# Last feature rows of the plain steps from one slot, spread copies placed in other steps, and shape order of odd tiles in a spectral-plus-MLP layer

## Chip, core and metric

The kernel runs on one core of a Trainium2 chip. The metric is the device time of one launch in microseconds; of several runs the median counts. The engines are TensorE (PE; its weight loads are listed apart as PEld), VectorE (DVE), ScalarE (ACT), GpSimd (POOL), and SyncE (SP), whose queue issues the transfers.

## What is computed

`x` has 2048 rows of 576 features, all in float32. Cut to what matters:

```python
x = A_x                                         # (1, 2048, 576)
X = rfft2(layernorm(x)) * (w_r + 1j * w_i)      # over rows and features
h = x + irfft2(X, s=(2048, 576))
h2 = h + relu(layernorm(h) @ w1) @ w2           # w1: 576 x 4608, w2: 4608 x 576
```

## The kernel before

The two-dimensional transform is written as products with constant matrices. The rows are split into 16 tiles of 128 rows, and the work runs in stages.

**Stage one** takes a tile `t` at a time. DVE measures mean and variance (`stat1`, `aggr1`, `row1`), POOL raises the variance to the power -0.5 (`pow1`), DVE and POOL fold the tile into sums and differences (`add1`, line 263, on DVE; `sub1`, line 258, on POOL), ACT scales the constants by the tile's deviation (`scale1`: line 267 writes one column, line 268 the 192 columns of constants), and PE multiplies (`fwd_a`): eight products of 128x128 and then four of 64x64 (`rest`). ACT evicts the result (line 159). The helpers `mm` and `act` record every product as line 156 and every copy or scaling on ACT as line 159. Tile 15 alone does its 64x64 products first, into a PSUM buffer of its own that DVE evicts (line 285). The loop runs over 18 steps; `fwd_a` follows two steps behind the statistics, so that in the order of ACT the scaling of a tile stands behind the eviction of the tile two before it.

**Stage two** (`mid_*`) does the small transforms and the spectral multiplication. **Stage three** goes back (`inv_*`), adds `x` (line 519), normalises again (`stat2`, `norm2`), and `project(t)` transposes each normalised tile, which makes the operands of the MLP. Its order is written out by hand in `STEPS`: a letter names a function, the number its argument, `A` and `B` are the two halves of a plain MLP step, and steps with `=` are jobs of a queue of sums and transfers.

The MLP works in float32 products of rounded high and low parts: w*x is taken as wh*xh + wh*xl + wl*xh. The rows are in four chunks of 512 (`CH` = 4 tiles), whose operands lie in `xc[c]` (tiles named B for chunks 0 and 1, C for chunk 2, X for chunk 3), with ten slots of 512 columns. The 576 features are 4 x 128 + 64, and slot 2 holds the 64 left over: their high part in partitions 0 to 63, the low part in 64 to 127. **Plain steps** (`mm1`, then `mm2`) take one group of 256 hidden units and one chunk. In `mm1` each 128 hidden units take 14 products: twelve for four blocks of 128 features and two for the last 64, one of which reads slot 2 and one slot 5. Slot 5 is filled by copies inside the chip, and they also move 32 partitions within slot 2: the last `project` of a chunk issues on SP four copies (line 579) and, behind their landing, a fifth (line 580). The **double steps** later on (Strassen's scheme over groups and chunk pairs, `l1_prod`, `second`, `slot`) read slots 0 to 2 and 3 to 5 as the two halves of the features.

Plain steps 3 to 8 run in a loop over `i` and `q`, with the table `JOBS` for what else is issued at each place (`L` loads, `S` sums, `H`, `I`, `W`, `X` splits, `K` stores). The first weights of the double steps are loaded by `load_w1` (lines 333 and 335) and `load_w2`; POOL makes their low parts (line 353) and the Strassen sums (lines 749 to 752).

## Time and profile before

| | before |
|---|---|
| median of 3 runs | 965.67 us (965.51 to 966.04) |
| profiled execution | 965.46 us |
| its span, first to last instruction | 963.7 us |
| busy: PE, PEld | 955.7 us (99%), 850.1 us (88%) |
| busy: DVE, ACT, POOL | 770.6 (80%), 466.7 (48%), 646.1 us (67%) |
| chain that ended last, by engine | PE 96%, DVE 1%, DMA 1%, ACT 1%, the rest under 1% |
| granted clock of TensorE, mean | 0.999 of full speed |

Between the span and the execution's own time lie 1.8 us. The busy share of an engine counts every instruction from its start to its end; the chain is followed back from the last instruction to what released it, step by step. A busy PE may still hold small gaps between its instructions, which the timeline shows.

### The profile page before, as it was taken

The page shows a single profiled execution, that of the slowest core. Times are in us where ns is not written, and L with a number is a line of the kernel's source. Part 1 is how long each engine was busy: PE and PEld are TensorE (multiplying, and loading weights), DVE is VectorE, ACT ScalarE, POOL GpSimd, SP SyncE. Part 2 cuts the span into 40 slices and gives each one's busy share as a digit, 9 for nine tenths or more (in the row PEclk, how much of TensorE's full clock was granted, in tenths as well). Part 3 has the DMA queues.
Part 4 walks back from the last instruction along what each step waited for, and adds up shares of the span by engine and source line. Part 5 has one row for each costly group of instructions (what it writes and reads, how often), then busy time and mean ns, then how long its engine had stood idle before and what let it go on. Part 6 is the DMA issues. An engine that isn't in the chain of part 4 may idle for free.

```text
span 963.7 us, 18094 instructions
## 1 busy us (share of the span) xinstructions
PE 955.7 (99%) x6658; PEld 850.1 (88%) x6658; DVE 770.6 (80%) x1226; ACT 466.7 (48%) x912; POOL 646.1 (67%) x783
## 2 busy tenths in 40 slices
PE   9999999999999999999999999999999999999997
PEld 7777778999988999999999999999999999999997
DVE  8577996687768888887888888888878888878886
ACT  6544558323355454545445444554554545444441
POOL 7213787514788777878686878767787768687842
PEclk9999999999999999999999999999999999999999
DMA  7974727557639264563728091836456372819365
GB/s 205 237 188 111 183 97 261 170 205 256 212 118 326 90 238 145 185 199 129 257 71 302 29 325 45 284 98 231 152 176 207 122 262 66 303 35 318 103 213 154
DMA packets 122840, 176.09 MB, mean 183 GB/s; under 512 B 7552, under 2 KB 102400, under 8 KB 122752
## 3 DMA queue, kind: packets, MB, share of 16 engines
q1 hardware_dynamic: 121584, 173.61, 55.9%
q10 hardware_dynamic: 1168, 1.33, 0.4%
q8 instruction: 53, 0.87, 0.4%
q14 instruction: 35, 0.29, 0.1%
HBM read 150.53 MB, written 23.07 MB: 180 GB/s over the span
## 4 chain that ended last, share of the span: by engine, by line
PE 96%; DVE 1%; DMA 1%; ACT 1%; issue 0%; SPq 0%; POOL 0%
PE h L826 36%; PE d L931 35%; PE d L156 24%; DMA C<-C 1%; PE d L564 1%; PE h L931 0%; DMA X<-in_A_x_dram 0%; DVE st L242 0%; ACT X L159 0%; ACT e L159 0%; ACT C L159 0%; DVE A L941 0%; DVE e L414 0%; DVE e L415 0%; DVE A L937 0%
## 5 line engine op out<-in xcount | busy, mean ns | idle before, releaser
L941 DVE TENSOR_TENSOR A<-A,d 128x576 f32<-128x576 f32 x428 | 317.5, 752 | 84.1 <-PE d L931 71.2
L931 PE MATMUL d<-X,D 128*128 128x288 f32 x1476 | 224.3, 294 | 0.1
L931 PEld LDWEIGHTS d<-X,D 128*128 128x128 f32 x1476 | 211.0, 188 | 10.5 <-DVE A L941 0.3
L826 PE MATMUL h<-B,e 128*128 128x512 f32 x658 | 166.8, 392 | 0.0
L159 ACT ACTIVATE e<-h 128x512 f32<-128x512 f32 x93 | 55.6, 597 | 188.0 <-PE h L826 187.9
L826 PEld LDWEIGHTS h<-B,e 128*128 128x128 f32 x658 | 118.3, 188 | 20.4
L353 POOL TENSOR_TENSOR e<-e,e 128x512 fp32r<-128x512 f32 (+3 forms) x68 | 89.8, 1320 | 57.9 <-ACT e L159 55.3
L642 ACT ACTIVATE e<-e 128x512 f32<-128x512 f32 x93 | 58.8, 633 | 107.5 <-DVE e L884 45.2
L826 PE MATMUL h<-X,e 128*128 128x512 f32 x434 | 110.0, 392 | 0.0
L353 POOL TENSOR_TENSOR X<-e,X 128x576 fp32r<-128x576 f32 (+1 forms) x34 | 49.9, 1469 | 62.8 <-ACT X L159 60.7
L826 PEld LDWEIGHTS h<-X,e 128*128 128x128 f32 x434 | 78.0, 188 | 13.4
L159 ACT ACTIVATE e<-e 128x256 fp32r<-128x256 f32 (+5 forms) x171 | 78.6, 489 | 14.3 <-DVE e L673 6.1
L850 POOL TENSOR_TENSOR A<-e 128x256 f32<-128x256 f32 x61 | 48.0, 787 | 28.4 <-DVE X L840 25.3
L840 DVE TENSOR_TENSOR D<-A,D 128x512 fp32r<-128x512 f32 x61 | 63.3, 1038 | 1.7 <-ACT D L159 1.7
L931 PEld LDWEIGHTS d<-X 128*128 128x128 f32 x372 | 55.6, 188 | 5.3 <-issue 0.4
L931 PE MATMUL d<-X 128*128 128x288 f32 x372 | 58.9, 294 | 0.1
L931 PE MATMUL d<-X,e 128*128 128x288 f32 x360 | 57.1, 294 | 0.0
L826 PE MATMUL h<-F,e 128*128 128x512 f32 x217 | 55.0, 392 | 0.0
L852 POOL TENSOR_TENSOR A<-e,A 128x256 f32<-128x256 f32 x61 | 52.9, 867 | 0.8 <-DVE A L848 0.8
L156 PE MATMUL d<-e,D 128*128 128x288 f32 x384 | 53.3, 295 | 0.0
L826 PE MATMUL h<-C,e 128*128 128x512 f32 x210 | 53.3, 393 | 0.0
L156 PEld LDWEIGHTS d<-e,D 128*128 128x128 f32 x384 | 51.9, 188 | 1.4 <-DVE A L632 0.4
(174 smaller groups left out, 1850.9 us busy)
## 6 DMA issues: line engine op xcount, KB each, us to landing
X<-t0T SPq DMA_DIRECT2D x16, 768.0 KB
X<-t1T SPq DMA_DIRECT2D x16, 768.0 KB
e<-in_B_w_dram SPq DMA_DIRECT2D x18, 576.0 KB
e<-in_B_w_dram SPq DMA_DIRECT2D x18, 512.0 KB
X<-t0T SPq DMA_DIRECT2D x16, 512.0 KB
X<-t1T SPq DMA_DIRECT2D x16, 512.0 KB
B<-t1T SPq DMA_DIRECT2D x8, 768.0 KB
B<-t1B SPq DMA_DIRECT2D x8, 768.0 KB
```

The lines of the kernel that those rows point to most:

```text
L156: nc.tensor.matmul(o, l, r, start=start, stop=stop)
L159: nc.scalar.activation(o, i, AF.Copy, **kw)
L353: eng.tensor_sub(l, v, h)
L564: nc.tensor.transpose(pz[:, 128 * ORDER[b]:128 * ORDER[b] + 128], y[:, 128 * b:128 * b + 128], ident)
L642: nc.scalar.activation(o, i, AF.Relu)
L826: nc.tensor.matmul(o, a, b, start=bool(first) and n_ == 0, stop=n_ == len(ops) - 1, skip_group_check=not first)
L840: (eng or nc.vector).tensor_sub(f[1], v, f[0])
L850: nc.gpsimd.tensor_sub(s3, p0[:, :256], p0[:, 256:])
L852: nc.gpsimd.tensor_sub(s4, p1_[:, :256], s2)
L931: nc.tensor.matmul(P[tt], l[:, q], r, start=first and n_ == 0, stop=end and n_ == 2, skip_group_check=whole and not first)
L941: nc.vector.tensor_add(xt, xt, P)
```

## The change

Four places are edited. (1) In stage one the odd tiles issue their 64x64 products ahead of the 128x128 ones. (2) The last tile's statistics, fold and scaling are issued in step 15 of the loop instead of step 16, and its subtraction by DVE instead of POOL. (3) The two products of `mm1` for the last 64 features both read slot 2; the weights of these features are therefore loaded twice, into partitions 0 to 63 and 64 to 127, their high part is made by one copy on ACT, and the low part is followed by zeros. That takes two transfers instead of three and no memset. Group 2 (`FIRST`), which serves plain and double steps, loads both forms. (4) The spread copies leave `project` and become jobs: `F0`, `F1`, `F3` fill slot 5 of a chunk, `G0` moves the 32 partitions within slot 2 of chunk 0, and the five copies of chunk 2 are issued at step (`END` - 1, 2). `project` is told which engine takes its 64-row subtraction: POOL for tiles 0 to 7, DVE for the others (before, tiles 3 and 7 were DVE's too).

```diff
@@ -22,6 +22,7 @@
 GF = 2
 NG = DFF // (128 * GF)
 CH = 4
+FIRST = 2
 NC = NT // CH
 WARM = 25
 APART = 3
@@ -254,8 +255,8 @@
         r = first(t)[4]
         nc.gpsimd.tensor_tensor(r[:, 1:2], r[:, 0:1], half[:, :1], op=ALU.pow)
 
-    def sub1(t):
-        nc.gpsimd.tensor_sub(dims(first(t)[0], 575, [1, 2], [-2, 144]), *pair(t))
+    def sub1(t, eng=nc.gpsimd):
+        eng.tensor_sub(dims(first(t)[0], 575, [1, 2], [-2, 144]), *pair(t))
 
     def add1(t):
         G, _, _, _, r = first(t)
@@ -283,13 +284,15 @@
             p2 = ps()
             rest(p2)
             nc.vector.tensor_copy(dims(zx, 8192 + 2 * t, [32, 64], [1, 2]), dims(p2, 256, [1, 64], [512, 2]))
+        elif t % 2:
+            rest(p)
         for h in range(2):
             for k in range(2):
                 for j in range(2):
                     q = slice(64 * j, 64 * j + 64)
                     mm(p[:, 512 * j + 128 * h:512 * j + 128 * h + 128], dims(G[q], (k, 321 - k)[h], [2, 128]),
                        caf[q, 64 * k:64 * k + 128], k == 0, k == 1)
-        if not end:
+        if t % 2 == 0:
             rest(p)
         act(dims(zx, 2 * t, [2048, 5 - end], [32, 64], [1, 2]), dims(p, 0, [64, 5 - end], [1, 64], [512, 2]))
 
@@ -301,7 +304,7 @@
     warm_pe(WARM)
     sub1(0)
     for t in range(NT + 2):
-        old = 1 <= t <= NT
+        old = 1 <= t < NT
         if old and t <= 2:
             row1(t - 1)
             pow1(t - 1)
@@ -315,12 +318,18 @@
             stat1(t, 1)
         if old and t > 2:
             add1(t - 1)
-        if 1 <= t < NT:
+        if 1 <= t < NT - 1:
             sub1(t)
         if t < NT:
             aggr1(t)
-        if old:
+        if 1 <= t < NT:
             scale1(t - 1)
+        if t == NT - 1:
+            row1(t)
+            pow1(t)
+            add1(t)
+            sub1(t, nc.vector)
+            scale1(t)
         if t >= 2:
             fwd_a(t - 2)
 
@@ -328,9 +337,16 @@
     nc.sync.dma_start(c3t, c3)
     raw, wts = {}, {}
 
+    def load_rest(g, v):
+        for k in range(2):
+            nc.sync.dma_start(v[64 * k:64 * k + 64], w1[512:576, 256 * g:256 * g + 256])
+
     def load_w1(g, v1, v4):
         f = slice(256 * g, 256 * g + 256)
         nc.sync.dma_start(v1, w1[0:512, f].rearrange("(a p) f -> p a f", p=128))
+        if g < FIRST:
+            load_rest(g, v4)
+            return
         for k in range(3):
             nc.sync.dma_start(v4[32 * k:32 * k + 32], w1[512:576, f].rearrange("(h p) f -> p h f", p=32))
 
@@ -368,9 +384,12 @@
         rest = [v[:, 1024:] for v in r]
         wts[g, 0] = h, l, rest
         v1, _, v4 = raw[g]
+        if g == FIRST:
+            v4 = vs["v4"]
         split(h, l, v1, nc.gpsimd)
-        for k in range(2):
-            split_rest(rest[k], v4[:, k], nc.gpsimd)
+        act(rest[0], v4)
+        nc.gpsimd.tensor_sub(rest[1][:64], v4[:64], rest[0][:64])
+        nc.gpsimd.tensor_sub(rest[1][64:], rest[0][64:], rest[0][64:])
 
     def split_rest(o, v, eng=nc.vector):
         act(o, v)
@@ -462,7 +481,7 @@
         if step[0] == "l":
             mid_l(k, k + 1)
         elif step[0] == "L":
-            load_weights(0, leftover())
+            load_weights(0, sb([128, 512], "G")[:, :256])
         elif step[0] == "W":
             warm_pe(k)
         else:
@@ -557,7 +576,7 @@
             nc.scalar.activation(z[:, i, :D], xs[:, t0 + i, :], AF.Identity, bias=r[2][:, 2, i:i + 1], scale=r[2][:, 1, i:i + 1])
         act(z[:, :, D:], z[:, :, 512:D])
 
-    def project(t):
+    def project(t, eng):
         y = Zs.pop(t)
         pz = ps()
         for b in range(5):
@@ -571,20 +590,20 @@
         nc.sync.dma_start(xd[t], zt)
         for h in range(2):
             nc.gpsimd.tensor_sub(dst[:, 6 + 2 * h:8 + 2 * h, q], zt[:, 384 * h:384 * h + 256].rearrange("p (a s) -> p a s", s=128), dst[:, 3 * h:3 * h + 2, q])
-        made[t // CH] += 1
-        (nc.gpsimd if t < 8 and made[t // CH] < CH else nc.vector).tensor_sub(dst[64:, 2, q], zt[64:, 256:384], dst[64:, 2, q])
-        if made[t // CH] == CH:
-            u = dst.bitcast(F32)
+        eng.tensor_sub(dst[64:, 2, q], zt[64:, 256:384], dst[64:, 2, q])
+
+    def spread(c, half):
+        u = xc[c].bitcast(F32)
+        if half:
             for a, b in ((0, 32), (32, 32), (64, 96), (96, 96)):
                 nc.sync.dma_start(u[a:a + 32, 5], u[b:b + 32, 2])
+        else:
             nc.sync.dma_start(u[32:64, 2], u[0:32, 2])
 
     ORDER = (0, 1, 3, 4, 2)
-    made = [0] * 4
     xd = {}
     hid, pend = {}, {}
     steps = [(0, 0), (0, 1), (0, 2), (1, 1), (0, 3), (1, 3), (1, 0), (1, 2), (2, 3), (2, 2)]
-    FIRST = 2
     END = len(steps) - 1
 
     ring = []
@@ -606,7 +625,7 @@
         for kt in range(4):
             x = kt + kt // 2
             ops += [(w1h[:, kt, f], x), (w1h[:, kt, f], 6 + kt), (w1l[:, kt, f], x)]
-        ops += [(rest[h][:, f], 3 * h + 2) for h in range(2)]
+        ops += [(rest[h][:, f], 2) for h in range(2)]
         for n_, (w, x) in enumerate(ops):
             mm(p, w, xc[c][:, x, :], n_ == 0, n_ == len(ops) - 1)
         if i < APART:
@@ -1057,17 +1076,15 @@
         "h1 h0 S1 d1 o1 d0 o0 S0 h3 h9 d9 d3 r1 h2 e0 h6 e1 h4 s0 s1 d4 o3 d2 d6 n0 o6 h10 o2 h7 d10 d7 j1 o7 r2 "
         "e2 h11 h5 h12 e3 s2 s3 d5 j0 o4 o5 d12 d11 r4 n2 h13 e6 e7 d13 s6 o10 j2 o11 j3 h8 r3 e5 e4 h14 d8 d14 "
         "s7 s4 s5 r6 e11 o9 h15 n6 o12 o14 o13 d15 A0 o8 e10 n4 A1 o15 j6 s10 j4 j5 B0 r5 e9 r7 e8 e13 e12 j7 "
-        "s11 B1 B2 s8 s9 r8 e15 s12 =K0 n10 e14 s14 T n8 s13 B3 A10 =L0 j10 A11 j9 j11 j8 B10 s15 n12 =L1 B11 V0 "
-        "B12 B13 n14 =P0 j13 j12 A20 =S0 V1 A21 j14 A30 =S1 j15 =L2 =L3 A31 B20 =P1 B21 =H0 B22 =W0 =H1 B23 =W1 "
-        "=S2 "
+        "s11 B1 B2 s8 s9 r8 e15 s12 =F0 =F1 =K0 n10 e14 s14 T n8 s13 B3 A10 =L0 J10 A11 J9 J11 J8 B10 s15 n12 =L1 "
+        "B11 V0 B12 B13 n14 =P0 J13 J12 A20 =S0 V1 A21 J14 A30 =S1 J15 =L2 =L3 A31 B20 =P1 =F3 B21 =H0 B22 =W0 =H1 "
+        "B23 =W1 =S2 "
     )
 
     def tail_in():
         tail.append(sb([128, 10752], "X", dt=F32R))
         xc.append(tail[0][:, :5120].rearrange("p (a n) -> p a n", a=10))
-        v4 = ebuf([128, 2, 256])
-        nc.gpsimd.memset(v4, 0.0)
-        load_weights(1, v4)
+        load_weights(1, ebuf([128, 256]))
         groups.extend(sum_jobs(k // CH, k % CH, v) for k, v in enumerate("ABCABABA"))
 
     groups, stage, FT = [], [], {}
@@ -1089,20 +1106,20 @@
 
     JOBS = (
         "L4 / H2 I0 I1 / W2 X0 X1 / S3 L5 I2 / X2 H3 I3 / W3 X3 K1 / S4 L6 / "
-        "H4 I4 / W4 X4 / S5 L7 / H5 I5 / W5 X5 / S6 / H6 I6 / W6 X6 / S7 / H7 I7 / W7 / X7"
+        "H4 I4 / W4 X4 / S5 L7 / H5 I5 / W5 X5 / S6 / G0 H6 I6 / W6 X6 / S7 / H7 I7 / W7 / X7"
     ).split(" / ")
 
     def job(name, k):
         if name in "LSHIWX":
             groups[k][name]()
         else:
-            dict(K=keep_block, P=sum_bufs)[name](k)
+            dict(K=keep_block, P=sum_bufs, F=lambda c: spread(c, 1), G=lambda c: spread(c, 0))[name](k)
 
     def work(k):
         for v in JOBS[k].split() if 0 <= k < len(JOBS) else ():
             job(v[0], int(v[1:]))
 
-    CALLS = dict(h=inv_h, d=inv_d, o=inv_o, r=inv_r, e=inv_e, s=stat2, n=lambda t: norm2(t, 2), j=project,
+    CALLS = dict(h=inv_h, d=inv_d, o=inv_o, r=inv_r, e=inv_e, s=stat2, n=lambda t: norm2(t, 2), j=lambda t: project(t, nc.gpsimd), J=lambda t: project(t, nc.vector),
                  A=lambda k: mm1(*divmod(k, 10)), B=lambda k: mm2(*divmod(k, 10)), T=lambda k: tail_in(),
                  S=lambda k: split_weights(0, k), V=lambda k: split_weights(1, k))
     for step in STEPS.split():
@@ -1126,7 +1143,10 @@
                 TF["T4"] = TS[:, 0:3], TS[:, 3:5]
             work(4 * i + q - 12)
             if (i, q) == (4, 3):
-                vs[1], vs[2], vs[4] = raw[FIRST] = ebuf([128, 4, 256]), ebuf([128, 2, D]), leftover()
+                e = ebuf([128, EW])
+                vs["v4"] = e[:, 1024:]
+                vs[1], vs[2], vs[4] = raw[FIRST] = e[:, :1024].rearrange("p (a b) -> p a b", a=4), ebuf([128, 2, D]), leftover()
+                load_rest(FIRST, vs["v4"])
                 load_w1(FIRST, vs[1], vs[4])
             if (i, q) == (5, 2):
                 load_w2(FIRST, vs[2])
@@ -1141,6 +1161,9 @@
                 w2_sums()
             if (i, q) in ((END - 2, 3), (END - 1, 0)):
                 w2_split(("T34", "T12")[q == 3], nc.gpsimd)
+            if (i, q) == (END - 1, 2):
+                spread(2, 1)
+                spread(2, 0)
             if i == END - 1:
                 if q == 0:
                     w1_sums(0)
```

Three places in the order of the instructions follow, before and after. The first is PE in stage one, tiles 0 to 3; `d` is the tile's PSUM buffer, `e` its folded rows.

```order
L156 MATMUL d_236<-e_200 128x128 x8
L156 MATMUL d_236<-e_200 64x64 x4
L156 MATMUL d_264<-e_212 128x128 x8
L156 MATMUL d_264<-e_212 64x64 x4
L156 MATMUL d_292<-e_226 128x128 x8
L156 MATMUL d_292<-e_226 64x64 x4
L156 MATMUL d_320<-e_250 128x128 x8
L156 MATMUL d_320<-e_250 64x64 x4
```

After the change, at the same place:

```order
L157 MATMUL d_236<-e_200 128x128 x8
L157 MATMUL d_236<-e_200 64x64 x4
L157 MATMUL d_264<-e_212 64x64 x4
L157 MATMUL d_264<-e_212 128x128 x8
L157 MATMUL d_292<-e_226 128x128 x8
L157 MATMUL d_292<-e_226 64x64 x4
L157 MATMUL d_320<-e_250 64x64 x4
L157 MATMUL d_320<-e_250 128x128 x8
```

Only the two pieces of the odd tiles (d_264, d_320) have changed places; the tiles themselves keep their order.

The second is ACT at the end of stage one, before. `A<-d` is an eviction (of tiles 12 to 15 here), `e<-X,r` and `e<-cc,r` are the two scalings of a tile (14 and 15).

```order
L159 ACTIVATE A_173<-d_572 128x320x2
L267 ACTIVATE e_558<-X_66,r_86_561 128x1
L268 ACTIVATE e_558<-cc_76,r_86_561 128x192
L159 ACTIVATE A_173<-d_600 128x320x2
L267 ACTIVATE e_586<-X_66,r_91_589 128x1
L268 ACTIVATE e_586<-cc_76,r_91_589 128x192
L159 ACTIVATE A_173<-d_620 128x320x2
L159 ACTIVATE A_173<-d_634 128x256x2
```

And after:

```order
L160 ACTIVATE A_173<-d_572 128x320x2
L268 ACTIVATE e_558<-X_66,r_86_561 128x1
L269 ACTIVATE e_558<-cc_76,r_86_561 128x192
L268 ACTIVATE e_586<-X_66,r_91_589 128x1
L269 ACTIVATE e_586<-cc_76,r_91_589 128x192
L160 ACTIVATE A_173<-d_606 128x320x2
L160 ACTIVATE A_173<-d_620 128x320x2
L160 ACTIVATE A_173<-d_634 128x256x2
```

The scaling of tile 15 (e_586) now stands ahead of the eviction of tile 13 (d_600 before, d_606 after).

The third is SP's queue, at the two places between which the copies of chunk 2 move. `x` is a store of a transposed tile, `X<-x` a load for the sums, `X<-t0T` a load of stored sums, `e` and `G` are the weights of the next group. Before, the earlier place:

```order
L571 DMA x_2184<-e_2181 128x640
L571 DMA x_2198<-e_2195 128x640
L579 DMA C_1417<-C_1417 32x512 x4
L580 DMA C_1417<-C_1417 32x512
L666 DMA X_2070<-x_1591 128x2x256
L669 DMA X_2070<-x_1591 128x1x128 x2
```

After, the later place (there, before the change, L333 followed directly on the loads X<-t0T):

```order
L735 DMA X_2065<-t0T_2485 128x4x384
L735 DMA X_2065<-t0T_2485 128x4x256
L599 DMA C_1415<-C_1415 32x512 x4
L601 DMA C_1415<-C_1415 32x512
L346 DMA e_2761<-in_B_w_dram 128x4x256
L351 DMA G_2763<-in_B_w_dram 32x2x256 x3
```

The four copies and the fifth stand some 65 places further down the queue, ahead of the weights.

## Rows read from the trace of the kernel before

**Rows 1.** The page: the span, and PE's busy time, share and instructions.

```profile
span 963.7 us, 18094 instructions
...
PE 955.7 (99%) x6658; PEld 850.1 (88%) x6658; DVE 770.6 (80%) x1226; ACT 466.7 (48%) x912; POOL 646.1 (67%) x783
```

**Rows 2.** Waits of PE's weight loads: line, releaser, total us, times, longest us.

```profile
PEld d L156 <- ACT e L268: 1.4, 3, 0.6
...
PEld d L156 <- DMA C<-C: 0.5, 1, 0.5
```

**Rows 3.** Timeline of ACT, end of stage one: start, us, instruction, idle before.

```profile
26.45 0.75 ACT L159 ACTIVATE A<-d 128x640 f32<-128x640 f32 x1 [0.17 <-PE d L156]
...
27.28 0.44 ACT L268 ACTIVATE e<-cc,r 128x192 f32<-128x192 f32 x1
...
28.69 0.45 ACT L268 ACTIVATE e<-cc,r 128x192 f32<-128x192 f32 x1
29.32 0.74 ACT L159 ACTIVATE A<-d 128x640 f32<-128x640 f32 x1 [0.18 <-PE d L156]
```

**Rows 4.** Timeline of PE's weight loads: tile 14's 64x64, then tile 15's.

```profile
28.91 0.15 PEld L156 LDWEIGHTS d<-e 64*64 64x64 f32 x4
...
28.91 0.21 PEld L156 LDWEIGHTS d<-e 64*64 64x64 f32 x8
...
29.19 0.21 PEld L156 LDWEIGHTS d<-e 64*64 64x64 f32 x8
```

**Rows 5.** Timelines of DVE (tiles 11, 14, 15) and POOL (tile 15).

```profile
22.09 0.51 DVE L263 SCALAR_TENSOR_TENSOR e<-X,r 128x288 f32<-128x288 f32 x1
...
26.12 0.51 DVE L263 SCALAR_TENSOR_TENSOR e<-X,r 128x288 f32<-128x288 f32 x1
27.17 0.53 DVE L263 SCALAR_TENSOR_TENSOR e<-X,r 128x288 f32<-128x288 f32 x1
...
27.25 0.85 POOL L255 TENSOR_TENSOR r<-r,half 128x1 f32<-128x1 f32 x1
```

**Rows 6.** Timelines of SP, PEld, PE and DVE around the first step on chunk 2.

```profile
156.88 2.51 SPq L579 DMA_DIRECT2D C<-C  x4
161.95 0.51 SPq L580 DMA_DIRECT2D C<-C  x1
...
163.93 1.22 PEld L156 LDWEIGHTS d<-C,F 128*128 128x128 f32 x6 [0.50 <-DMA C<-C]
...
160.87 6.98 PE L156 MATMUL d<-C,F 128*128 128x512 f32 x28
...
181.54 3.38 PE L156 MATMUL d<-X,F 128*128 128x512 f32 x14
...
156.88 0.45 DVE L575 TENSOR_TENSOR C<-e,C 64x128 fp32r<-64x128 f32 x1 [0.99 <-ACT C L159]
```

**Rows 7.** Timelines of DVE and PEld around tile 3's 64-row subtraction.

```profile
121.67 0.43 DVE L575 TENSOR_TENSOR B<-e,B 64x128 fp32r<-64x128 f32 x1
...
123.60 0.69 PEld L156 LDWEIGHTS d<-X,cc 64*64 64x64 f32 x14 [0.33 <-DVE A L519]
```

**Rows 8.** Timeline of SP: the copies of chunk 1.

```profile
140.46 2.41 SPq L579 DMA_DIRECT2D B<-B  x4
```

**Rows 9.** SP's timeline, DMA view of 254:260, POOL's timeline.

```profile
252.09 2.12 SPq L716 DMA_DIRECT2D X<-t0T  x2
259.81 0.39 SPq L333 DMA_DIRECT2D e<-in_B_w_dram  x1
...
DMA packets 1639, 2.26 MB, mean 377 GB/s; under 512 B 69, under 2 KB 1383, under 8 KB 1639
...
264.14 0.73 POOL L353 TENSOR_TENSOR e<-e,e 128x256 fp32r<-128x256 f32 x1 [2.37 <-DMA G<-in_B_w_dram]
...
271.13 1.29 POOL L353 TENSOR_TENSOR e<-e,e 128x512 fp32r<-128x512 f32 x1 [0.91 <-ACT e L159]
...
275.36 1.44 POOL L353 TENSOR_TENSOR X<-e,X 128x576 fp32r<-128x576 f32 x1 [2.13 <-issue]
```

## The prediction

> **What bounds the kernel now.** The page comes first: the span is 963.7 us and TensorE is busy for 955.7 of it [rows 1], so a change pays only where it takes away PE work (there is none of that here: products and their shapes are the same) or a moment in which PE stands still. So the next view is the waits of PE's weight loads, and of those the two that the change can touch: the scaled constants of stage one, ACT e L268, and the landing of the copies C<-C [rows 2]. The timeline then shows how much of either is lost, and which engine sets the pace around it. The change touches four places. I take them in program order.
>
> **1. Odd tiles of stage one.** The edit puts an odd tile's 64x64 products next to the 64x64 products of the even tile ahead of it, so PE changes tile shape once per tile instead of twice. Whether this pays depends on who holds PE. On ACT the eviction of tile 12 starts at 26.45, the scaling for tile 14 ends at 27.28 + 0.44 = 27.72, and the eviction of tile 14 starts at 29.32 [rows 3]: a loop of 2.87 us for two tiles, from an eviction through the scaling behind it and PE's tile to that tile's own eviction. PE does not start when it is free: the scaling for tile 15 ends at 28.69 + 0.45 = 29.14 [rows 3], and tile 15's first load stands at 29.19 [rows 4], 0.05 behind. Odd and even tiles have a loop each, interleaved on ACT. In the even loop the PE part is the same eight 128x128 products followed by four 64x64, before and after; the shape change that is saved lies between two tiles, in PE's idle time. So I take nothing for tiles 1 to 13. Bounds: nothing, or that all pay (rival 1).
>
> **2. The end of stage one.** Here the order on ACT changes: the scaling for tile 15 goes ahead of the eviction of tile 13. DVE's add for tile 15 ends at 27.17 + 0.53 = 27.70 and POOL's power at 27.25 + 0.85 = 28.10 [rows 5]; the subtraction moves to DVE behind the add, and I take 0.5 for it, as the add, so it ends at 28.2. The scaling can follow that of tile 14 (27.72) and ends between 28.34 (0.18 + 0.44 behind it) and 28.55 (0.45 behind the power, should that not start earlier). Tile 15 is then no longer waited for but waits for PE: tile 14's 64x64 loads stand at 28.91 in two groups 0.06 apart (the four cover 0.15, the eight 0.21 [rows 4]), so the next group fits at 28.91 + 0.11 = 29.02. Tile 15 starts at 29.02 instead of 29.19: **-0.17**. The price on the other side is the eviction of tile 13, which now starts at about 28.5 and ends (0.74) by 29.25, before the next eviction's 29.32 [rows 3]: no cost, with 0.07 to spare; should it be late, it takes back at most that 0.17. The other bound is a gain of 0.3, if the last eviction follows as well. What follows in stage two is bound by PE, and I carry the gain over unreduced.
>
> **3. Slot 2 instead of slot 5 in the plain steps.** A mm1 step ended in a product that read slot 5, filled by the spread copies. For chunk 2 they came late: four copies issued from 156.88, the fifth only when they had landed, at 161.95, and PE's load at 163.93 stands behind 0.50 of idle for C<-C [rows 6]. The first mm1 on chunk 2 and its neighbour take 6.98 for 28 products; undisturbed a step of 14 takes 3.38 [rows 6]. Below, the loss is 6.98 - 2 x 3.38 = 0.22, since this counts the tail of the first step, which overlaps the second, twice; above, it is the whole 0.50. I take the middle: **-0.36**. After the change both last products read slot 2 of chunk 2, and the last thing that writes it is the subtraction of DVE at 156.88, done at 157.33, three and a half microseconds before the step begins at 160.87 [rows 6]. So nothing is late next.
>
> The doubled weight rows cost PE nothing (same products and shapes). POOL's two 64-row subtractions take the place of two of 32 rows, and its memset goes; SP issues two transfers for three. All of this is behind work that PE does not wait for: among its waits the only transfer is C<-C [rows 2].
>
> **4. Subtractions and copies that move.** For tiles 3 and 7 the 64-row subtraction goes from DVE to POOL. The first stood on DVE at 121.67 for 0.43, just ahead of the additions for which PE then waits 0.33 at 123.60 [rows 7]. Bounds are 0 (the additions wait for PE's own products anyway) and 0.33; a third of that is **-0.10**. The copies of chunks 0 and 1 become eight in front of the stores of slot blocks; four of them took 2.41 on SP at 140.46 [rows 8], and SP waited besides, for the fifth copies and for POOL's memset, which both go; so I take nothing, with 2.41 of later loads as the bound, and none of these is waited for by PE [rows 2].
>
> The copies of chunk 2 move behind two loads X<-t0T. On SP these end at 252.09 + 2.12 = 254.21, and the next issue, for the weights of the following group, is at 259.81, when its buffer comes free [rows 9]. By the earlier place the pair holds SP for 161.95 + 0.51 - 156.88 = 5.58, that is until 259.79: it just fits. But the queue is full there: 2.26 MB move from 254 to 260 at 377 GB/s [rows 9], and copies behind them land about when those are through, at 260, plus their own 0.33 MB (five of 32x512 words of 4 bytes), 0.9 us, so that SP would be free only at about 261.5. That is 7.3 instead of 5.58, and the weights go out 1.7 late. POOL takes them up at 264.14 and then idles 0.91 before 271.13 and 2.13 before 275.36 [rows 9]: 3.04 of slack cover it. **0**, as long as the pair takes less than 5.58 + 3.04 = 8.6.
>
> The Trainium skill speaks against this place: "DMA: Bandwidth & Descriptors", Queues, rings and completion order, has each DMA engine consume descriptors of a ring in order, so copies issued behind large loads start behind them; its section Anatomy of one DMA gives some 2.0 us fixed for a transfer, which would make the pair about 4 us by itself, an estimate. By the first of these the sum stays as above with the cover nearly used up, and by the second alone SP would be free at about 258. The trace agrees with the first at the old place, where the four copies took from 156.88 to 161.95 and not two.
>
> **The sum.** -0.17 - 0.36 - 0.10 = -0.63. The profiled execution took 965.46, which is 0.21 below the median of 965.67; 964.83 by that execution is 965.04 by the median. I predict **965.0 us**. About 0.2% (1.9 us) is what a measurement of this kernel can tell from no change, so the forecast lies within it.
>
> **The rivals.**
>
> *Rival 1, stage one runs freely.* If the ACT loop shortens as PE's tile gets shorter, the next pace is DVE's: its add comes at 22.09 and three tiles later at 26.12, 1.34 per tile [rows 5], against 1.43 on ACT. Fourteen tiles at 0.09 less are 1.26, in place of nothing: 965.04 - 1.26 = 963.8. For it: a shape change is a part of each tile's PE time. Against it: the even tiles' own order is untouched, and each start follows the scaling by 0.05. I give it 0.14. Where other stalls of the stage fall too it may pass 963.7.
>
> *Rival 2, slower: the copies at 254 hold SP.* One mechanism: the fifth copy of chunk 2 waits on SP for the landing of the other four, and the weights of the next group wait behind it. It decides when the pair takes longer than 8.6 us. At twice the old 5.58, 11.2, the loss is 11.2 - 8.6 = 2.6 on the chain through POOL, and the time 965.04 + 2.6 = 967.6. For it: the full queue. Against it: the copies are 0.33 MB, and the 2.26 MB are through by 260. I give it 0.08.
>
> *Rival 3, the change does nothing.* C<-C goes, but PE then waits for something next to it (ACT's or DVE's split of an earlier hidden block), and tile 15's gain ends in the wait for the last eviction. Then 965.5 to 965.7. For it: many small waits stand close together in stage three, such as that for DVE A L519 [rows 7]. I give it 0.17.
>
> **How the numbers follow.** The forecast has 0.60; rival 1 0.14, rival 3 0.17, rival 2 0.08, 0.01 is left. From the bounds of the terms the forecast's own range is 965.67 - (0.3 + 0.5 + 0.33) = 964.5 to 965.67 - 0.22 = 965.4. The range 963.4 to 966.2 takes in rivals 1 and 3 with about 0.5 for what the loads moved in stage three may add, and leaves out rival 2. Faster by over 0.2% (under 963.74) is most of rival 1's lower half and a little more: 0.12. Slower by over 0.2% (over 967.60) is the larger part of rival 2 and other late weights: 0.07. Within: 0.81.
>
> **What would show it.** Step 1: evictions of stage one still 1.43 apart, and odd tiles' first 64x64 loads 0.05 behind the scaling; 1.34 would be rival 1. Step 2: tile 15 starts about 29.02 with the scaling ahead of the eviction of tile 13. Step 3: no wait for C<-C in PE's list, 28 products in about 6.6 to 6.7. Step 4: no L575 row of DVE near 121.67; the copies C<-C on SP at about 254, the next weights' load by 261.5, and no PE wait between 270 and 300 that was not there before. A gap there, or evictions off their pace, would make the prediction wrong.

## The result and the profile after

The changed kernel takes 968.15 us as the median of 9 runs (966.82 to 971.47), the kernel before 965.65 us beside it (965.44 to 966.34): a ratio of 1.003 with a 95% interval of 1.0018 to 1.0041. It is slower by some 2.5 us, where 965.0 was forecast, and its runs scatter over 4.7 us, where those of before scatter over 0.9. The page of its profiled execution (969.8 us) has these lines against [rows 1]:

```profile
span 968.0 us, 18080 instructions
...
PE 955.9 (99%) x6658; PEld 850.5 (88%) x6658; DVE 773.1 (80%) x1225; ACT 465.4 (48%) x909; POOL 644.6 (67%) x782
```

PE's work is as before to 0.2 us, and the span is 4.3 longer: all but that 0.2 is PE standing still. The waits of PE's weight loads say on whom (line, releaser, total us, times, longest us). C<-C, in [rows 2], is gone from the list, as forecast. PE's waits for the scaled constants of stage one (ACT e) have grown from 1.4 us in 3 [rows 2] to 2.9 in 9. New are an "issue" wait of 1.9 and two waits at L950, a line of the double steps, for POOL X L369 and ACT X L160.

```profile
PEld d L157 <- issue: 11.0, 24, 1.9
PEld d L157 <- ACT e L269: 2.9, 9, 0.7
PEld d L950 <- POOL X L369: 1.7, 1, 1.7
...
PEld d L950 <- ACT X L160: 0.9, 1, 0.9
```

To place them I set the start of each PE product beside that of the product with the same number in the trace of before. The table gives by how many us PE is late against before (negative: early) at places named by their time in before, for the changed kernel and for the experiments below. What lies ahead of the first column differs from run to run (the first rows of x land at other times, and in some traces one of DVE's adds takes 0.6 longer); only the steps between columns count.

```
PE in before at           28.0   29.7   95.3  102.0  122.0  126.2  163.5  164.5  270.2  278.2  290.1  958.0
after                     0.69   0.53   0.49   2.61   2.61   2.10   2.12   1.75   1.75   4.20   4.09   4.08
e1_early_four             0.40   0.23   0.20   2.24   2.24   1.73   1.75   1.39   1.38   1.38   1.38   1.36
e2_memset_kept           -0.05  -0.22  -0.25  -0.21  -0.21  -0.72  -0.70  -1.06  -1.06   1.19   1.09   1.06
e3_both                   0.15  -0.01  -0.05  -0.01  -0.01  -0.52  -0.53  -0.89  -0.89  -0.89  -0.90  -0.92
e4_before_early_memset    0.73   0.72   0.71   0.71   0.71   0.71   0.69   0.74   0.78   0.78   0.75   0.74
e5_w2_first               0.26   0.10   0.06   0.11   0.12  -0.39  -0.39  -0.75  -0.76  -0.76  -0.76  -0.78
e6_before_pool_subs       0.22   0.20   0.20   0.19   0.20  -0.30  -0.29   1.11   1.11   1.11   1.10   1.09
e7_scale_one_ahead       -0.15  -0.07  -0.05   0.00   0.01  -0.50  -0.51  -0.88  -0.88  -0.88  -0.89  -0.93
e8_scale_ahead_no_pairs   0.36   0.20   0.16   0.20   0.21  -0.30  -0.28  -0.64  -0.64  -0.64  -0.65  -0.67
e9_three_transfers        0.44   0.28   0.24   2.39   2.39   1.88   1.90   1.54   1.53   1.53   1.54   1.54
```

The changed kernel gains at three places: 0.16 at tile 15, 0.51 around 123, 0.37 at 164. It loses 2.12 around 98 and 2.34 around 278.

**The loss around 98.** First SP, ACT, POOL's low part of w2, DVE and PE's loads of the kernel before there:

```profile
85.33 1.27 SPq L335 DMA_DIRECT2D G<-in_B_w_dram  x3
86.70 1.54 SPq L343 DMA_DIRECT2D e<-in_B_w_dram  x1
88.29 17.34 SPq L481 DMA_DIRECT2D A<-in_A_x_dram  x16
...
91.87 1.16 ACT L159 ACTIVATE e<-e 128x1152 fp32r<-128x1152 f32 x1 [0.84 <-DMA e<-in_B_w_dram]
93.88 0.41 ACT L159 ACTIVATE e<-d 128x290 f32<-128x290 f32 x1 [0.84 <-PE d L156]
...
93.11 2.63 POOL L353 TENSOR_TENSOR e<-e,e 128x1152 fp32r<-128x1152 f32 x1 [5.19 <-ACT e L159]
...
95.30 0.76 DVE L544 TENSOR_TENSOR X<-e 128x289 f32<-128x289 f32 x1
...
98.08 0.69 PEld L156 LDWEIGHTS d<-X,cc 64*64 64x64 f32 x16
```

And the same in the changed kernel:

```profile
84.19 1.16 SPq L342 DMA_DIRECT2D G<-in_B_w_dram  x2
85.45 0.52 SPq L359 DMA_DIRECT2D e<-in_B_w_dram  x1
86.02 19.31 SPq L500 DMA_DIRECT2D A<-in_A_x_dram  x16
...
94.74 1.16 ACT L160 ACTIVATE e<-e 128x1152 fp32r<-128x1152 f32 x1 [3.22 <-DMA e<-in_B_w_dram]
95.81 0.70 ACT L160 ACTIVATE e<-d 128x290 f32<-128x290 f32 x2
...
95.98 2.63 POOL L369 TENSOR_TENSOR e<-e,e 128x1152 fp32r<-128x1152 f32 x1 [7.58 <-ACT e L160]
...
97.22 1.72 DVE L563 TENSOR_TENSOR X<-e 128x289 f32<-128x289 f32 x1
...
99.82 0.46 DVE L563 TENSOR_TENSOR X<-e 128x289 f32<-128x289 f32 x1
...
100.36 0.22 PEld L157 LDWEIGHTS d<-X,cc 64*64 64x64 f32 x4 [1.93 <-issue]
```

With the memset gone SP no longer waits ahead of the weight rows (84.19 here, 85.33 before), and the sixteen loads of x begin at 86.02 instead of 88.29. The load of w2 just ahead of them goes out earlier too, by 1.25, and yet it is there later: ACT's split of it (128x1152) waits until 94.74, against 91.87. Behind that split in ACT's order stand the evictions of the inverse transform (95.81 against 93.88), and on them hang DVE's additions (line 563, before line 544), whose sums PE multiplies next. The first of these takes 1.72 instead of 0.76: it ends 0.3 us after POOL's low part of w2 (95.98 + 2.63 = 98.61), as it did before (93.11 + 2.63 = 95.74), and that is now as late as the split. The second ends at 99.82 + 0.46 = 100.28, and PE's load starts at 100.36 (in e1 and e9, too, it follows by 0.07). PE's list shows this wait as "issue"; the transfer behind it stands only in ACT's row.

**The loss around 278** is rival 2. SP, ACT, POOL and PE's loads:

```profile
254.93 2.40 SPq L735 DMA_DIRECT2D X<-t0T  x2
257.37 2.70 SPq L599 DMA_DIRECT2D C<-C  x4
266.11 0.51 SPq L601 DMA_DIRECT2D C<-C  x1
266.73 0.52 SPq L346 DMA_DIRECT2D e<-in_B_w_dram  x1
...
270.69 0.42 ACT L160 ACTIVATE e<-e 128x256 fp32r<-128x256 f32 x1 [5.24 <-DMA e<-in_B_w_dram]
...
271.24 0.74 POOL L369 TENSOR_TENSOR e<-e,e 128x256 fp32r<-128x256 f32 x1 [7.71 <-ACT e L160]
...
277.73 1.31 POOL L369 TENSOR_TENSOR e<-e,e 128x512 fp32r<-128x512 f32 x1
...
279.92 1.46 POOL L369 TENSOR_TENSOR X<-e,X 128x576 fp32r<-128x576 f32 x1
...
279.57 0.19 PEld L950 LDWEIGHTS d<-X 128*128 128x128 f32 x1 [0.87 <-ACT X L160]
281.43 0.69 PEld L950 LDWEIGHTS d<-X 128*128 128x128 f32 x5 [1.68 <-POOL X L369]
```

By SP's waits and the landings in the trace the fifth copy stands behind the first two of the four, not behind all of them; these two are there at 265.88 and 266.04. The pair holds SP from 257.37 to 266.62, 9.25 us, and the weights go out at 266.73 against 259.81 [rows 9]: 6.92 later, of which PE's own lag of 1.75 is no loss, so 5.17 late. POOL's two idle times of [rows 9], 0.91 and 2.13, are gone (it runs from 271.24 to 282.25 without a gap), and 5.17 - 3.04 = 2.13 is what PE then waits, measured as 2.34. Counted at POOL's first row, 271.24 against 264.14 [rows 9], it is 7.10 - 1.75 - 3.04 = 2.31.

### The profile page after: what moved, and what is told of

It is laid out like the page before. It is cut to its first block, busy times and chain, and to the rows that moved or that the text cites. A ratio compares the mean times of both kernels' runs of the same rounds, so it can differ in the third digit from the quotient of the medians.

```text
span 968.0 us, 18080 instructions
## 1 busy us (share of the span) xinstructions
PE 955.9 (99%) x6658; PEld 850.5 (88%) x6658; DVE 773.1 (80%) x1225; ACT 465.4 (48%) x909; POOL 644.6 (67%) x782
## 4 chain that ended last, share of the span: by engine, by line
PE 96%; DVE 2%; issue 1%; DMA 0%; ACT 0%; POOL 0%; ACTq 0%
PE h L845 36%; PE d L950 35%; PE d L157 24%; PE d L583 1%; DVE st L243 1%; PE h L950 0%; DMA X<-in_A_x_dram 0%; ACT X L160 0%; DVE A L960 0%; DVE e L433 0%; DVE mv L247 0%; POOL X L369 0%; DVE e L434 0%; DVE r L251 0%; DVE A L956 0%
## 5 line engine op out<-in xcount | busy, mean ns | idle before, releaser
L950 PE MATMUL d<-X,D 128*128 128x288 f32 x1476 | 224.2, 294 | 0.1
L950 PEld LDWEIGHTS d<-X,D 128*128 128x128 f32 x1476 | 211.0, 188 | 10.5 <-DVE A L960 0.3
L160 ACT ACTIVATE e<-h 128x512 f32<-128x512 f32 x93 | 55.5, 597 | 186.1 <-PE h L845 186.0
L369 POOL TENSOR_TENSOR e<-e,e 128x512 fp32r<-128x512 f32 (+3 forms) x68 | 89.8, 1320 | 62.8 <-ACT e L160 62.6
L160 ACT ACTIVATE e<-e 128x256 fp32r<-128x256 f32 (+6 forms) x172 | 79.0, 489 | 25.7 <-DMA e<-in_B_w_dram 8.5
L369 POOL TENSOR_TENSOR X<-e,X 128x576 fp32r<-128x576 f32 (+1 forms) x34 | 49.9, 1468 | 60.9 <-ACT X L160 60.9
L950 PEld LDWEIGHTS d<-X 128*128 128x128 f32 x372 | 55.5, 188 | 7.8 <-POOL X L369 1.7
L950 PE MATMUL d<-X 128*128 128x288 f32 x372 | 59.3, 294 | 2.1 <-POOL X L369 1.5
L950 PE MATMUL d<-X,e 128*128 128x288 f32 x360 | 57.1, 294 | 0.0
```

What stands on the lines that cost most here:

```text
L160: nc.scalar.activation(o, i, AF.Copy, **kw)
L369: eng.tensor_sub(l, v, h)
L950: nc.tensor.matmul(P[tt], l[:, q], r, start=first and n_ == 0, stop=end and n_ == 2, skip_group_check=whole and not first)
```

## The experiments

**Each loss undone by itself, and both.** Three kernels made from the changed one. In `e1_early_four` the four copies go to the place of `G0`:

```diff
-S5 L7 / H5 I5 / W5 X5 / S6 / G0 H6 I6
+S5 L7 / H5 I5 / W5 X5 / S6 / G0 F2 H6 I6
...
             if (i, q) == (END - 1, 2):
-                spread(2, 1)
                 spread(2, 0)
```

> The changed kernel, but the four copies of chunk 2 that fill slot 5 are issued together with the one copy of chunk 0 (where SP stands idle from 232.7 to 237.2 in the changed kernel's trace); only the fifth copy stays ahead of the weights at 257. Theory: in the changed kernel the pair held SP from 257.37 to 266.62 (9.25 us), the weights went out 5.05 us late against the PE offset, POOL's 3.04 us of slack were used up and PE lost 2.2 us at 277 to 281. Then the weights here are out by about 259 to 262, both PE waits there are gone, and the time is about 2.2 below the changed kernel's 968.15: 966.0. Rival: the weights are late because the queue is full of X<-t0T, whoever stands in it; then the waits stay and the time stays at 968. The stall of 1.8 us at 98 should be as it was under both.

Measured: 966.24 us (964.52 to 968.98, 11 runs) against 965.72 of before; ratio 1.0006, 0.9997 to 1.0015. The table has no step at 278, and SP's rows are these, with ACT's at the other place:

```profile
256.98 0.84 SPq L601 DMA_DIRECT2D C<-C  x1
261.20 0.39 SPq L346 DMA_DIRECT2D e<-in_B_w_dram  x1
...
94.35 1.16 ACT L160 ACTIVATE e<-e 128x1152 fp32r<-128x1152 f32 x1 [3.12 <-DMA e<-in_B_w_dram]
```

The weights go out at 261.20, which is their time before and PE's lag (259.81 + 1.38). The same loads X<-t0T stand ahead (issued from 254.58), and one copy behind them costs nothing: it is the wait of one copy for others, on SP, that made the loss. The step at 98 is there unchanged (2.04 in the table).

`e2_memset_kept` puts the memset back for group 0:

```diff
-            load_weights(0, sb([128, 512], "G")[:, :256])
+            g0 = sb([128, 512], "G")
+            nc.gpsimd.memset(g0, 0.0)
+            load_weights(0, g0[:, :256])
```

> The changed kernel, but POOL's memset ahead of the loads of the last 64 weight rows of group 0 is put back. Theory: without it SP issues the sixteen x loads 2.3 us earlier (86.02 instead of 88.29), they share the queue with the load of w2 just ahead of them, ACT's split of w2 waits for it (3.22 of idle, until 94.74 instead of about 91.9), the evictions behind it on ACT are late, and PE stands still 1.8 us at 98. Then with the memset the x loads go out at about 88, the split starts at about 92 to 92.5, the PE wait at 98 is gone, and the time is about 1.8 below 968.15: 966.4. Rival: POOL's order there (the split of w2 ahead of the subtraction X L562), or a late start of that run, made the stall; then it stays, and the time is 968.

Measured: 966.64 us (965.65 to 969.20); ratio 1.0011, 1.0002 to 1.002. The x loads go out late, w2's split starts early, and the step at 98 is gone; that at 278 stays (2.25), with the pair at 254.54 and 263.18:

```profile
87.99 4.56 SPq L502 DMA_DIRECT2D A<-in_A_x_dram  x7
...
91.25 1.16 ACT L160 ACTIVATE e<-e 128x1152 fp32r<-128x1152 f32 x1 [0.47 <-DMA e<-in_B_w_dram]
...
254.54 2.64 SPq L601 DMA_DIRECT2D C<-C  x4
263.18 0.51 SPq L603 DMA_DIRECT2D C<-C  x1
```

`e3_both` has both edits.

> The changed kernel with both edits: four copies of chunk 2 early, memset kept. If both losses are as said and independent, the time is that of the prediction without them, 965.0 to 965.4, a little below before, and its runs scatter less than the changed kernel's 966.8 to 971.5. If either theory fails it is 966 to 968.

Measured: 964.72 us (964.27 to 966.00); ratio 0.9991, 0.9982 to 1.0. That is 1.00 below before by the medians. Against the kernel before beside them the medians are +2.50 for the changed kernel, +0.52 for e1, +0.92 for e2 and -1.00 here. So keeping the memset takes away 1.58 with the pair as it is and 1.52 with the four copies moved, and moving these takes away 1.98 and 1.92: the two losses add. Both are thus shown to be what was said, and what is left of the change is a gain, at the edge of what the interval tells (those of e5, e7 and e8 below lie under 1).

**Is it the x loads, or the order at w2?** `e4_before_early_memset` is the kernel before with the memset earlier. It runs at 70.34 instead of 84.78, so the 30 us in the expectation are 14:

```diff
+    v40 = leftover()
     for step in "d11 b10 l12 d12 b11 d13 i9 b12 l14 b13 d14 i10 b14 d15 i11 L b15 i12 i13 i14 i15".split():
...
-            load_weights(0, leftover())
+            load_weights(0, v40)
```

> The kernel before with one edit: POOL's memset for group 0 is issued some 30 us earlier, so that SP need not wait for it ahead of the loads of the last 64 weight rows (83.70 to 85.33 in the trace of before). Theory of the collision: the x loads go out about 1.6 us earlier (86.7 instead of 88.3), w2 lands later, ACT's split waits for it to about 94, and PE loses 1 to 1.8 us at 98: 966.7 to 967.5. Rival (the stall belongs to other parts of the change): no stall, and the time is 965.6 or a little less.

Measured: 965.70 us (ten of 11 runs 965.18 to 966.22, one 969.17) against 965.72; ratio 1.0003, 0.9994 to 1.0012. This is the rival's time: the x loads went out at 86.40, and in the profiled run ACT waited only 0.75 for w2 and PE not at all. Early x loads alone need not cost anything:

```profile
92.50 1.16 ACT L159 ACTIVATE e<-e 128x1152 fp32r<-128x1152 f32 x1 [0.75 <-DMA e<-in_B_w_dram]
```

`e5_w2_first`, made from `e1_early_four`, keeps them early and puts w2 ahead of w1:

```diff
-        load_w1(g, v1, v4)
-        load_w2(g, v2)
+        if g == 0:
+            load_w2(g, v2)
+        load_w1(g, v1, v4)
+        if g:
+            load_w2(g, v2)
```

> The changed kernel with the four copies of chunk 2 early and without the memset, as e1_early_four, but the load of w2 of group 0 is issued ahead of its w1 instead of behind it. Theory: the loss of 1.8 us at 98 arises only because the last of the sixteen parts of w2 lands up to 5 us late when the x loads run beside it; issued first, w2 is through before the x loads begin, ACT's split does not wait, and the time is that of e3_both, 964.7, with as little scatter. Should w1 now be the straggler, its split on ACT at about 95 waits instead and the time is 965.5 to 966.5. Rival (the x loads as such, early, cost the time through another engine): the time stays at 966.2.

Measured: 964.80 us (964.33 to 965.17); ratio 0.999, 0.9981 to 0.9999. SP issues w2 at 83.32, the x loads still start at 85.88, and ACT's split waits for no transfer:

```profile
83.32 0.39 SPq L359 DMA_DIRECT2D e<-in_B_w_dram  x1
...
85.88 6.13 SPq L503 DMA_DIRECT2D A<-in_A_x_dram  x7
...
90.99 1.16 ACT L160 ACTIVATE e<-e 128x1152 fp32r<-128x1152 f32 x1
```

So it is through w2's landing, and through nothing else, that the early x loads cost time. `e9_three_transfers` asks why e4 escaped; it is `e1_early_four` with three transfers ahead of w2:

```diff
-        for k in range(2):
-            nc.sync.dma_start(v[64 * k:64 * k + 64], w1[512:576, 256 * g:256 * g + 256])
+        for a, n in ((0, 64), (64, 32), (96, 32)):
+            nc.sync.dma_start(v[a:a + n], w1[512 + a % 64:512 + a % 64 + n, 256 * g:256 * g + 256])
```

> As e1_early_four (no memset, w2 behind w1), but the last 64 weight rows go in three transfers, of 64, 32 and 32 rows, instead of two of 64. e4_before_early_memset, which also let the x loads start early but with three transfers ahead of w2, hardly ever stalled, e1_early_four in most runs. Theory A: what counts is how many transfers and bytes stand ahead of w2 and the x loads in the queue; with three transfers w2's last part lands by about 92.5 and the time is that of e3_both, 964.7. Theory B: the early x loads alone make one of w2's sixteen parts late, by chance, and e4's runs were lucky; then the times scatter as those of e1_early_four, about a median of 966.

Measured: 965.63 us (964.66 to 966.94); ratio 0.9997, 0.9988 to 1.0006. Runs as low as those of `e3_both` stand beside runs 2 us above. Its profiled run (966.82) is one with the stall (2.15 in the table, ACT's split at 94.51). Theory A fails: three transfers ahead of w2 do not bring it in time. Theory B holds in that w2 is late in some runs and in time in others. That e4 escaped by luck is not shown: six of the 11 runs here lie 0.9 or more above the median of `e3_both`, and ten of e4's 11 within 0.6 of the kernel before. What spares e4 stays open.

**The gain around 123.** `e6_before_pool_subs` is the kernel before with the subtractions of tiles 3 and 7 on POOL:

```diff
-        (nc.gpsimd if t < 8 and made[t // CH] < CH else nc.vector).tensor_sub(dst[64:, 2, q], zt[64:, 256:384], dst[64:, 2, q])
+        (nc.gpsimd if t < 8 else nc.vector).tensor_sub(dst[64:, 2, q], zt[64:, 256:384], dst[64:, 2, q])
```

> The kernel before with one edit: the 64-row subtractions of tiles 3 and 7 go from DVE to POOL. All traces of the changed kernels show PE 0.50 us earlier behind the place at 123.4 to 123.6, where DVE's additions (L519 of before) no longer stand behind a subtraction of 0.43. Theory: that edit alone gives the 0.50, so 965.2 by the median, and PE's wait of 0.33 at 123.60 goes or falls below 0.1. Rival: the copies moved away from SP or the lighter POOL gave it; then the trace shows the wait as before and the time stays at 965.7.

Measured: 966.53 us (965.78 to 967.70) against 965.76; ratio 1.0007, 0.9999 to 1.0016. The gain of 0.50 is there (0.20 to -0.30 in the table) and is taken back almost threefold at 164. POOL, SP and PE's loads show how:

```profile
142.36 0.46 POOL L575 TENSOR_TENSOR B<-e,B 64x128 fp32r<-64x128 f32 x1
...
140.17 3.82 SPq L579 DMA_DIRECT2D B<-B  x4
...
157.68 2.84 SPq L579 DMA_DIRECT2D C<-C  x4
...
165.04 2.12 PEld L156 LDWEIGHTS d<-C,F 128*128 128x128 f32 x10 [1.91 <-DMA C<-C]
```

On POOL tile 7's subtraction waits its turn until 142.36, where DVE did it at 140.47. The copies of chunk 1 wait for it on SP (3.82 instead of 2.41, [rows 8]), everything behind them is late, and the copies of chunk 2 go out at 157.68 instead of 156.88 [rows 6]; PE's wait for C<-C grows from 0.50 to 1.91. In the changed kernel no product waits for these copies, so the same edit gives its 0.5.

**Stage one's pace.** In `e7_scale_one_ahead`, made from `e3_both`, PE follows one tile later, so that the loop from an eviction over the scaling back to an eviction spans three tiles; `e8_scale_ahead_no_pairs` does without the new order of the odd tiles as well.

```diff
-    for t in range(NT + 2):
+    for t in range(NT + 3):
...
-        if t >= 2:
-            fwd_a(t - 2)
+        if t >= 3:
+            fwd_a(t - 3)
```

> The kernel of e3_both, but in stage one PE's tile follows three steps behind the statistics instead of two, so that ACT scales a tile's constants ahead of the eviction of the tile three before it. Theory: what sets stage one's pace is the loop eviction, scaling, PE's tile, eviction (2.86 us for two tiles, 1.43 a tile, in every trace so far); over three tiles the same loop allows under 1.0, the pace falls to DVE's 1.34 or a little below, and some 13 tiles save 0.09 or more each: 1.0 to 1.3 us less than e3_both, 963.5. Rival: PE or DVE already holds the stage; then the evictions stay 1.43 apart and the time stays at 964.7.

> As e7_scale_one_ahead, but odd tiles do their 64x64 products last again, as in the kernel before. Theory: with the loop through ACT gone, PE's own changes of tile shape may count, at some 0.2 us for two tiles; if PE is then below DVE's pace of 1.34 in both, this equals e7_scale_one_ahead within 0.2 us; if PE's time per tile (about 1.42 for two shape changes by the 2.84 that two tiles took on PE) sets the pace, it is 0.5 to 1.2 us slower than e7_scale_one_ahead, and the pairing of shapes pays only here.

Measured: 964.63 us (964.02 to 964.93) and 964.62 us (964.22 to 964.91); ratios 0.9988 (0.9979 to 0.9997) and 0.9987 (0.9978 to 0.9995). The theory's first half holds: evictions of e7 come 1.34 apart, DVE's pace. Its second half, a gain of 1.0 to 1.3, fails: the time is that of `e3_both` to 0.1. Rows of ACT and DVE of e7:

```profile
13.05 0.71 ACT L160 ACTIVATE A<-d 128x640 f32<-128x640 f32 x1
14.39 0.71 ACT L160 ACTIVATE A<-d 128x640 f32<-128x640 f32 x1
...
27.79 0.52 DVE L264 SCALAR_TENSOR_TENSOR e<-X,r 128x288 f32<-128x288 f32 x1
```

The end of the stage hangs on the last tile, and that on DVE's own sequence, whose adds come 1.34 apart before the change as well [rows 5], whatever ACT and PE do. The last add stands at 27.79 here, at 27.32 in e3's trace and at 27.17 before; most of the difference is that one add of e7 took 1.13 (at 16.63) where the others took some 0.50. A faster loop mostly makes the tiles ahead of the last one done earlier. Something may be gained behind the last add: PE at 29.7 is 0.06 earlier than in `e3_both` though the last add is 0.47 later; but the medians show no more than 0.1. The pairing of shapes gives nothing in either setting.

## Why the prediction failed

Point by point, by its own steps.

**1, odd tiles: right.** Zero was forecast. Evictions of the changed kernel still come 2.86 apart for two tiles (first two rows below). What PE saves it stands waiting for the scaling, nine times instead of three. And e7 against e8 shows no difference of the order even with the loop gone. Rival 1 is refuted, and e7 shows a flaw in it besides: at DVE's pace the kernel would not have been its 1.26 faster either.

**2, the end of stage one: right, size too.** Forecast -0.17; PE goes from 0.69 late to 0.53, and by 0.16 or 0.17 in each kernel made from the changed one that keeps the two-step lag. ACT's rows show the scaling of tile 15 (28.31, 28.64) ahead of the eviction of tile 13 (29.00):

```profile
24.28 0.75 ACT L160 ACTIVATE A<-d 128x640 f32<-128x640 f32 x1 [0.24 <-PE d L157]
...
27.14 0.75 ACT L160 ACTIVATE A<-d 128x640 f32<-128x640 f32 x1 [0.26 <-PE d L157]
...
28.31 0.28 ACT L268 ACTIVATE e<-X,r 128x1 f32<-128x1 f32 x1
28.64 0.46 ACT L269 ACTIVATE e<-cc,r 128x192 f32<-128x192 f32 x1
29.00 0.71 ACT L160 ACTIVATE A<-d 128x640 f32<-128x640 f32 x1
```

**3, slot 2: the gain right, its cover wrong.** The 28 products take 6.61, against 6.98 in [rows 6]; forecast -0.36, measured -0.37. That the wait goes is as reasoned; that the size fits so well is luck, for it was the middle between 0.22 and 0.50.

```profile
162.99 6.61 PE L157 MATMUL d<-C,F 128*128 128x512 f32 x28
```

The first step that failed stands right behind it: "All of this is behind work that PE does not wait for: among its waits the only transfer is C<-C". I read PE's waits for transfers from PE's own list. That names the last releaser only, and ACT, which stands at the head of the chain that releases PE here, had itself waited 0.84 for w2 before the change. An edit that frees SP (no memset to wait for) was costed at nothing; it let x run into w2, and cost 2.12 in the profiled run and 1.5 to 1.6 by the medians.

**4, moved subtractions: sign right, size wrong.** Forecast -0.10, measured -0.51: the upper bound of 0.33 counted only the wait that PE's list names. Before, two of sixteen loads stand ahead of that wait and fourteen behind it [rows 7], from 123.08 to 123.60 + 0.69 = 124.29, which is 1.21; now the sixteen take 0.69 in one piece, 0.52 less:

```profile
123.08 0.19 PEld L156 LDWEIGHTS d<-X,cc 64*64 64x64 f32 x2
...
125.69 0.69 PEld L157 LDWEIGHTS d<-X,cc 64*64 64x64 f32 x16
```

**4, moved copies: the step that failed is "0, as long as the pair takes less than 8.6".** The chain and its slack were right (5.17 late, 3.04 of slack, 2.13 worked out, 2.34 measured in the profiled run, 1.9 to 2.0 by the medians); the 7.3 for the pair was not, nor was its start. The pair took 9.25, which by the condition alone costs only 9.25 - 8.6 = 0.65. It also began at 257.37, 1.41 later than the forecast 254.21 and PE's lag of 1.75 make, and the condition had no term for that. I had let the four copies land when the 2.26 MB of the stretch up to 260 were through, and the first two landed only 8.7 after the first was issued. But what moves in a stretch is not what is queued: by the landings in the trace of before, the second of the two loads X<-t0T ahead of that place was there only at 261.34. The rule of the Trainium skill quoted there ("DMA: Bandwidth & Descriptors", Queues, rings and completion order) pointed this way, and the trace agrees: the sixteen parts of that load landed from 262.87 to 265.71, and those of the first copy behind it from 263.20 to 265.88. The 2.0 us that the Trainium skill's section Anatomy of one DMA on that page has as fixed is stated for transfers that GpSimd issues; a copy from SP with nothing ahead of it fits it, as the fifth did before the change (issued at 161.95, PE's load at 163.93 [rows 6]). Rival 2, at 0.08 and priced at 2.6, named this mechanism and was given too little: the margin against it, 1.3 us, was smaller than the error of the estimate that it rested on.

**The sum.** The three gains add to -0.16 - 0.51 - 0.37 = -1.04, more than the forecast 0.63, and `e3_both`, which has them alone, lies 1.00 below before by the medians. The two losses add 2.12 and 2.34 in the profiled run. That run lies 1.65 above the median of its kernel, so in most of the others a loss must have been smaller, as the medians of the experiments say (1.5 to 1.6 and 1.9 to 2.0). The scatter of e1 and e9, which have only the first, shows that this one comes and goes.

**What stays open.** Why w2 is late in one run and not in the next was not settled: the trace does not say which of the sixteen parts of a transfer waits for what. That x follows closely is not enough: in the traces of e4 and e7 it does so too, and there w2 is not late enough to cost anything (last section). Nor was it settled why the pair of copies began later than PE's lag explains.

## What to carry to other kernels

An edit that frees a queue moves everything behind it forward, into the transfers that are under way: before costing it at nothing, follow the transfers that then overlap to the engine that waits for them, and on to what stands behind that wait in the engine's order, one hop further than PE's own list of waits. Do not put a copy whose issue waits for another copy's landing ahead of loads with a due time; split the pair, so that the first part lands long before. Where two changes are made at once, one may be worth something only because the other took away what it delays, as with the subtractions of tiles 3 and 7.

## What the runs showed of the hardware

A transfer signals in sixteen parts, and one of them can lie far behind the rest. By the landings in the traces, w2's parts landed as follows (us; first, last but one, last):

```
before                  90.96  91.67  91.79   x loads issued 1.59 behind w2
e2_memset_kept          90.70  91.10  91.17   1.69 behind
after                   89.20  92.38  94.66   0.57 behind
e9_three_transfers      88.98  92.03  94.43   0.43 behind
e4_before_early_memset  89.36  91.91  92.42   0.43 behind
e7_scale_one_ahead      89.74  90.34  91.44   0.59 behind
```

In the changed kernel, with x close behind, the first part landed earlier than before and the last 2.9 later; the last two rows show that x can be as close without this. Of the four copies inside the chip the first two landed 8.7 us after the first was issued at 257.37, with the loads X<-t0T just ahead of them in the queue; at 156.88 the fifth could go out after 5.1 [rows 6].

DVE's addition at line 563 (before, line 544) reads no PSUM buffer and takes 0.46 at the median of its 16 times. Started beside POOL's low part of w2, of 2.63 us, it ended 0.3 us after that, in the traces of before, after, e1, e4 and e9. DVE's additions that read a PSUM buffer (line 555) took 0.46 beside the same work of POOL in the changed kernel (at 96.24).
